# Transposing two token tiles by queue transfers set among the token loads, and the first tile's transposes by halves

## The chip, the cores and the metric

The kernel runs on one core of one Trainium2 chip. The metric is the device time of one execution in microseconds (us). The kernel before takes 1292.09 us (median of 3 runs, 1291.95 to 1292.39). Its granted TensorE clock is 1.000.

The engines are called as the profile calls them: PE is the matmul engine (TensorE), PEld its weight loads, DVE the vector engine, ACT the scalar engine, and SPq the sequencer that issues the transfers. "Landing" is the moment at which a transfer's data are complete.

## The reference, cut to what matters

```python
x = A_x                                                    # 2048 tokens x 1024, bf16
x = x + _A_ref(_layernorm(x), A_wqkv, A_wo)                # attention over 8 dilated positions, 32 heads
x = x + _B_ref(_layernorm(x), B_w1, B_b1, B_w2, B_b2)      # token-mixing MLP, 3584 wide
x = x + _A_ref(_layernorm(x), A_wqkv, A_wo)                # the same two again
x = x + _B_ref(_layernorm(x), B_w1, B_b1, B_w2, B_b2)
# in _A_ref:  qkv = x @ wqkv ; ... ; o @ wo
```

Only the opening of the first attention block matters here: the tokens are loaded, normalised over their 1024 features, transposed so that the features lie on the partitions, and multiplied with the value part of `wqkv`.

## The kernel before: the parts that matter

There are 16 token tiles of 128 tokens, called k. A list per engine gives the order of the opening's operations. `x_load` and `w_load` are loads of 256 KB each; `S_`, `A_` are the statistics on DVE; `R_` the reciprocal root on ACT; `N_` the normalisation on DVE. A tile is transposed either by PE (`tr`, eight 128x128 transposes into PSUM, followed by two ACT copies `C_` into `hT`) or by one queue transfer that transposes (`T_`). `V_` is the projection, 16 matmuls a tile, and `E_` the ACT copy of its result.

```python
        def tr(k):
            tps[k] = psm.tile([P, KD, P], BF16, name="m", tag="m")
            for kt in range(KD):
                r = nc.tensor.transpose(tps[k][:, kt, :], (xc[k] if k < 2 else xs[k])[:, kt * P:(kt + 1) * P], ident[:])
            return r

        def C_(k, hf):
            ks = slice(hf * KD // 2, (hf + 1) * KD // 2)
            return nc.scalar.copy(out=hT[:, ks, cols(*order[k])], in_=tps[k][:, ks, :])

        def T_(k):
            return nc.sync.dma_start_transpose(out=hT[:, :, cols(*order[k])], in_=xs[k])
        # ... [cut] all loads are issued first: x0, x1, w0..w3, x2, w4, w5, x3, w6, w7, x4 ... x15
        pe = [(tr, 0), (W_, 1), *VV(0, 0), (tr, 1), *VV(0, 1, 2), *VV(1, 0, 1, 2)]
        for kt in range(3, 6):
            pe += [*VV(0, kt), *VV(1, kt)]
        pe += [(tr, 2), *VV(0, 6, 7), *VV(1, 6, 7), (V_, 2, 0, a8), (tr, 3), (V_, 2, 1, a8), (tr, 4)]
        pe += [(V_, k, n, a8) for k in range(3, NT) for n in range(NDC)]
        # ... [cut]
        sp = [(T_, k) for k in (*range(np_, 10), 0, 1, *range(10, NT))] + [(load_biases,)]     # np_ = 5
```

So tiles 0 to 4 are transposed by PE, tiles 5 to 15 by the queue, after all loads. (Tiles 0 and 1 are only centred at first; the queue transposes them again later, scaled, for the query and key matmuls.) The queue's instructions run in the order of the list `sp`; a `T_` that waits for its normalisation holds up everything after it.

The softmax here doesn't subtract the row's maximum and nothing guards it: scores larger than these inputs give would overflow.

## Time and profile before

| | before |
|---|---|
| median, range | 1292.09 us, 1291.95 to 1292.39 (3 runs) |
| span of the profiled run | 1290.6 us |
| PE busy | 99% of the span |
| end of the opening (first query/key matmul, L383) | 64.32 us |

From the page: span, and busy time of each engine (share of the span, number of instructions).

```profile
span 1290.6 us, 19407 instructions
...
PE 1273.7 (99%) x8282; PEld 592.7 (46%) x8438; DVE 417.5 (32%) x854; ACT 370.9 (29%) x613; POOL 2.4 (0%) x15
```

PE is the bound. A change of the opening pays only if PE reaches the end of the opening earlier. The next lines are the timeline of PE (start, duration, engine, line, operation, out<-in, shape, how many; in brackets how long PE was idle before it and what ended that). Times of merged groups run to the end of the last matmul's pipeline, so they overlap a little; read the starts.

```profile
6.81 0.60 PE L267 MATMUL s<-wv,hT 128*128 128x512 bf16 x2 [0.46 <-ACT hT L261]
7.70 0.62 PE L256 MATMUL m<-ident,xc 128*128 128x128 bf16 x8 [0.29 <-DVE xc L238]
...
15.08 1.89 PE L267 MATMUL s<-wv,hT 128*128 128x512 bf16 x8
16.81 0.61 PE L256 MATMUL m<-ident,x 128*128 128x128 bf16 x8
17.25 1.89 PE L267 MATMUL s<-wv,hT 128*128 128x512 bf16 x8
18.98 0.61 PE L256 MATMUL m<-ident,x 128*128 128x128 bf16 x8
19.43 3.62 PE L267 MATMUL s<-wv,hT 128*128 128x512 bf16 x15
22.88 3.62 PE L267 MATMUL acc<-wv,hT 128*128 128x512 bf16 x16
...
64.32 7.07 PE L383 MATMUL m<-hT,wqk 128*128 128x512 bf16 x32
```

L256 is a PE transpose, L267 a projection matmul, L383 the first query/key matmul. Tile 3's transposes take 16.81 to 17.25 us and tile 4's 18.98 to 19.43 us; PE has no idle time near them (no bracket). The two small holes stand at the very start: before tile 0's projection (0.46 us) and before tile 1's transposes (0.29 us). Tile 4's projection, the first into the buffer `acc` after tile 1's, starts at 22.88 us.

The queue's side: the timeline of SPq.

```profile
7.57 8.54 SPq L219 DMA_DIRECT2D x<-in_A_x_dram  x12
22.21 24.16 SPq L279 DMA_TRANSPOSE hT<-x  x13
```

And from the view of line L279, the time from issue to landing of these 13 queue transposes.

```profile
DMA to landing us min/median/max: 3.0/3.6/5.0
```

All loads are issued by 16.1 us (7.57 + 8.54), and the first queue transpose follows at 22.21 us, just as the last load lands (22.24 us). It landed 3.2 us after issue.

### The profile page before, as it was taken

The page shows a single profiled execution, that of the slowest core. Times are in us where ns is not written, and L with a number is a line of the kernel's source. Part 1 is how long each engine was busy: PE and PEld are TensorE (multiplying, and loading weights), DVE is VectorE, ACT ScalarE, POOL GpSimd, SP SyncE. Part 2 cuts the span into 40 slices and gives each one's busy share as a digit, 9 for nine tenths or more (in the row PEclk, how much of TensorE's full clock was granted, in tenths as well). Part 3 has the DMA queues.
Part 4 walks back from the last instruction along what each step waited for, and adds up shares of the span by engine and source line. Part 5 has one row for each costly group of instructions (what it writes and reads, how often), then busy time and mean ns, then how long its engine had stood idle before and what let it go on. Part 6 is the DMA issues. An engine that isn't in the chain of part 4 may idle for free.

```text
span 1290.6 us, 19407 instructions
## 1 busy us (share of the span) xinstructions
PE 1273.7 (99%) x8282; PEld 592.7 (46%) x8438; DVE 417.5 (32%) x854; ACT 370.9 (29%) x613; POOL 2.4 (0%) x15
## 2 busy tenths in 40 slices
PE   9999999999999999999999999999999999999999
PEld 4444444444444444444444444444444444444444
DVE  6566777820000022322300677688000000111111
ACT  5366664541111110000023666645311111000000
POOL 0000000000000000000000000000000000000000
PEclk9999999999999999999999999999999999999999
DMA  6711123642222244465410111247423222334331
GB/s 223 112 46 48 50 83 124 208 139 82 66 82 75 57 117 132 132 165 131 132 32 1 48 49 51 80 150 219 116 66 92 71 61 82 100 106 138 116 92 33
DMA packets 201990, 126.07 MB, mean 98 GB/s; under 512 B 42160, under 2 KB 181680, under 8 KB 201904
## 3 DMA queue, kind: packets, MB, share of 16 engines
q1 hardware_dynamic: 201904, 124.82, 34.1%
q8 instruction: 66, 1.08, 0.3%
q14 instruction: 20, 0.16, 0.0%
HBM read 96.48 MB, written 16.78 MB: 88 GB/s over the span
## 4 chain that ended last, share of the span: by engine, by line
PE 98%; issue 1%; DMA 0%; DVE 0%; SPq 0%
PE m L383 17%; PE s L625 15%; PE s L578 15%; PE m L498 9%; PE acc L578 7%; PE m L578 7%; PE acc L625 7%; PE m L625 7%; PE m L368 4%; PE s L267 3%; PE s L414 2%; PE acc L267 1%; PE acc L449 1%; PE acc L453 1%; DMA x<-in_A_x_dram 0%
## 5 line engine op out<-in xcount | busy, mean ns | idle before, releaser
L625 PEld LDWEIGHTS <-w 128*128 128x128 bf16 x1820 | 177.0, 98 | 210.1
L578 PEld LDWEIGHTS <-w 128*128 128x128 bf16 x1792 | 175.3, 98 | 211.5
L383 PE MATMUL m<-hT,wqk 128*128 128x512 bf16 x963 | 223.3, 379 | 6.2 <-issue 4.6
L578 PE MATMUL s<-h,w 128*128 128x512 bf16 x878 | 201.2, 379 | 0.8
L625 PE MATMUL s<-g,w 128*128 128x512 bf16 (+1 forms) x912 | 201.0, 374 | 0.7
L627 DVE SCALAR_TENSOR_TENSOR xo<-s,b_sb,xs 128x512 bf16<-128x512 f32 (+1 forms) x33 | 24.4, 739 | 532.9 <-PE s L625 528.7
L383 PEld LDWEIGHTS <-wqk 128*128 128x128 bf16 x1024 | 95.2, 98 | 118.0 <-issue 10.7
L429 DVE TENSOR_TENSOR Pm<-pc,band 32x640 bf16<-32x640 bf16 x256 | 123.6, 483 | 56.2 <-ACT pc L417 49.4
L498 PE MATMUL m<-wo,oT 128*128 128x512 bf16 x500 | 110.6, 379 | 0.8 <-issue 0.3
L578 PE MATMUL acc<-h,w 128*128 128x512 bf16 x440 | 103.1, 379 | 0.5
L625 PE MATMUL acc<-g,w 128*128 128x512 bf16 x436 | 99.6, 379 | 0.5
L578 PE MATMUL m<-h,w 128*128 128x512 bf16 x438 | 98.5, 379 | 0.5
L625 PE MATMUL m<-g,w 128*128 128x512 bf16 (+1 forms) x436 | 96.9, 376 | 0.6
L176 ACT ACTIVATE ln<-mv,eps 128x1 f32<-128x1 f32 x64 | 18.9, 295 | 225.2 <-DVE mv L184 184.9
L498 PEld LDWEIGHTS <-oT 128*128 128x128 bf16 x512 | 49.6, 98 | 60.3 <-issue 1.3
L585 ACT ACTIVATE g<-s,b_sb 128x1024 bf16<-128x1024 f32 x28 | 31.2, 1114 | 158.2 <-PE s L578 146.4
L394 DVE COPY qB<-qs 32x512 bf16<-32x512 bf16 x136 | 38.2, 281 | 95.3 <-ACT qs L390 94.0
L368 PE MATMUL m<-wv,hT 128*128 128x512 bf16 x251 | 55.2, 379 | 0.3
L417 ACT ACTIVATE pc<-s,shift 128x640 bf16<-128x640 f32 x64 | 51.2, 800 | 11.7 <-PE s L414 11.7
L390 ACT CAST qs<-m 128x512 bf16<-128x512 f32 x64 | 37.5, 586 | 48.3 <-PE m L383 47.2
L387 ACT CAST kT<-m 128x512 bf16<-128x512 f32 x64 | 37.5, 586 | 46.4 <-PE m L383 46.4
L505 DVE TENSOR_TENSOR xn<-m,xr 128x512 bf16<-128x512 f32 x64 | 44.2, 690 | 16.9 <-PE m L498 16.4
(67 smaller groups left out, 683.0 us busy)
## 6 DMA issues: line engine op xcount, KB each, us to landing
w<-in_B_w_dram SPq DMA_DIRECT2D x56, 512.0 KB, 3.7
w<-in_B_w_dram SPq DMA_DIRECT2D x64, 448.0 KB, 4.4
wqk<-in_A_wqkv_dram SPq DMA_DIRECT2D x16, 512.0 KB, 5.2
xa<-xn SPq DMA_DIRECT2D x32, 256.0 KB, 2.2
xs<-xa SPq DMA_DIRECT2D x32, 256.0 KB, 3.1
wo<-in_A_wo_dram SPq DMA_DIRECT2D x8, 512.0 KB, 5.3
xr<-in_A_x_dram SPq DMA_DIRECT2D x16, 256.0 KB, 3.3
xb<-xo SPq DMA_DIRECT2D x16, 256.0 KB, 2.9
```

Of the source, the lines that this page charges most:

```text
L267: r = nc.tensor.matmul(pss_[k][:, n, :], lhsT=hT[:, kt, cols(*order[k])], rhs=wv[kt // 2][:, kt % 2, n * 512:(n + 1) * 512], start=(kt == ...
L368: nc.tensor.matmul(ps[:], lhsT=hT[:, kt, cols(c, i)], rhs=wv[kt // 2][:, kt % 2, n * 512:(n + 1) * 512], start=(kt == 0), stop=(kt == KD - 1))
L383: mm = nc.tensor.matmul(ps[:], lhsT=wts[part][:, kt, (g % 2) * P:(g % 2 + 1) * P], rhs=hT[:, kt, lo:lo + 512], start=(kt == 0), stop=(kt = ...
L387: nc.scalar.copy(out=kT[u % 2][:, ls], in_=ps[:])
L390: nc.scalar.copy(out=qs[:], in_=ps[:])
L394: nc.vector.tensor_copy(out=qB[u % 2][hp, h, ls], in_=qs[hp, :])
L417: nc.scalar.activation(out=pc[:].rearrange("p (n t) h k -> p n (t h k)", n=2), in_=ss[:, :, 0:2 * HG * GW], func=ACT.Exp, scale=scale, bia ...
L429: mm = nc.vector.tensor_tensor(out=Pm[rp, :, s0:s0 + HB, r * KG:r * KG + GW].rearrange("p h t k -> p t h k"), in0=pc[rp], in1=mk, op=ALU.mult)
L498: mm = nc.tensor.matmul(ps[:], lhsT=oT[g][:, cols(c, i)], rhs=wo[n][g // 4][:, g % 4, :], start=(g == 0), stop=(g == NG - 1))
L505: return nc.vector.tensor_tensor(out=xn[:, xs_], in0=pss_["o", n][:], in1=xr[:, xs_], op=ALU.add)
L578: nc.tensor.matmul(pairs[fl][0][dc], lhsT=wt[c][:, i, fl * P:(fl + 1) * P], rhs=h2[c][i][:, dc * 512:(dc + 1) * 512], start=(k == 0), stop ...
L625: nc.tensor.matmul(ap, lhsT=w2t[ft // HF][:, ft % HF, c::DIL], rhs=g[ft // GF][:, ft % GF, lo:lo + w], start=(ft == 0), stop=(ft == FT - 1))
```

## The change

The intent: tiles 3 and 4 leave PE too. Their queue transposes can't stand after all the loads, because PE would need the tiles before that, so they are set between the later loads. In passing, `tr` and `C_` go by halves with an own PSUM tile for each half, so that the copy of tile 0's first half need not wait for the transposes of its second. The diff, cut to its core:

```diff
@@ start_up
-        def tr(k):
-            tps[k] = psm.tile([P, KD, P], BF16, name="m", tag="m")
-            for kt in range(KD):
-                r = nc.tensor.transpose(tps[k][:, kt, :], ...)
+        def tr(k, hf):
+            tps[k, hf] = psm.tile([P, KD // 2, P], BF16, name="m", tag="m")
+            for j in range(KD // 2):
+                lo = (hf * KD // 2 + j) * P
+                r = nc.tensor.transpose(tps[k, hf][:, j, :], ...)
             return r
         def C_(k, hf):
-            return nc.scalar.copy(out=hT[:, ks, cols(*order[k])], in_=tps[k][:, ks, :])
+            return nc.scalar.copy(out=hT[:, ks, cols(*order[k])], in_=tps[k, hf][:])
@@ orders   [cut: the warm-up matmuls get a 128x128 tile of zeros that is filled first]
-        pe += [(tr, 2), *VV(0, 6, 7), *VV(1, 6, 7), (V_, 2, 0, a8), (tr, 3), (V_, 2, 1, a8), (tr, 4)]
-        pe += [(V_, k, n, a8) for k in range(3, NT) for n in range(NDC)]
+        pe += [(tr, 2, 0), (tr, 2, 1), *VV(0, 6, 7), *VV(1, 6, 7)]
+        pe += [(V_, k, n, a8) for k in range(2, NT) for n in range(NDC)]
-        act = [..., (R_, 2), (C_, 2, 0), (C_, 2, 1), (R_, 3), (E_, 0), (E_, 1), (R_, 4), (C_, 3, 0), (C_, 3, 1), (E_, 2),
-               (C_, 4, 0), (C_, 4, 1), (R_, 5), (E_, 3), (R_, 6)]
+        act = [..., (R_, 2), (R_, 3), (C_, 2, 0), (C_, 2, 1), (R_, 4), (E_, 0), (R_, 5), (E_, 1), (R_, 6), (E_, 2), (E_, 3)]
-        sp = [(T_, k) for k in (*range(np_, 10), 0, 1, *range(10, NT))] + [(load_biases,)]
+        sp = [(x_load, 0, halves), (x_load, 1), ...,   # as before up to
+              (x_load, 4), (x_load, 5), (x_load, 6), (T_, 3), (x_load, 7), (x_load, 8),
+              (T_, 4), (x_load, 9), (x_load, 10), (x_load, 11), (T_, 5), (x_load, 12), (x_load, 13), (T_, 6), (x_load, 14),
+              (x_load, 15), (T_, 7), (T_, 8), (T_, 9), (T_, 0), (T_, 1), *((T_, k) for k in range(10, NT)), (load_biases,)]
```

More of the change, by code (lines that the diff above doesn't have):

```diff
@@ L116 @@
     make_identity(nc, ident[:])
+    warm = const.tile([P, P], BF16, name="warm")
+    nc.vector.memset(warm[:], 0.0)
     eps1 = const.tile([P, 1], FP32, name="eps1")
@@ L206, in start_up @@
     def start_up(v, wv):
-        np_ = 5
         xc = [x2(f"xc{k}") for k in range(2)]
-        warm = x2("warm", [P, 512])
-        nc.vector.memset(warm[:], 0.0)
         xs, tps, pss_, mvs, sts, rss = {}, {}, {}, {}, {}, {}
@@ L251, in N_ @@
             return r
-        def tr(k):
-            tps[k] = psm.tile([P, KD, P], BF16, name="m", tag="m")
-            for kt in range(KD):
-                r = nc.tensor.transpose(tps[k][:, kt, :], (xc[k] if k < 2 else xs[k])[:, kt * P:(kt + 1) * P], ident[:])
+        def tr(k, hf):
+            tps[k, hf] = psm.tile([P, KD // 2, P], BF16, name="m", tag="m")
+            for j in range(KD // 2):
+                lo = (hf * KD // 2 + j) * P
+                r = nc.tensor.transpose(tps[k, hf][:, j, :], (xc[k] if k < 2 else xs[k])[:, lo:lo + P], ident[:])
             return r
@@ L279, in T_ @@
             return nc.sync.dma_start_transpose(out=hT[:, :, cols(*order[k])], in_=xs[k])
-        wm = m_tile()
+        wm = s_tile()
         def W_(n):
             for _ in range(n):
-                r = nc.tensor.matmul(wm[:], lhsT=warm[:, 0:P], rhs=warm[:], start=True, stop=True)
+                r = nc.tensor.matmul(wm[:, 0, :].rearrange("p (n q) -> p n q", q=P), lhsT=warm[:],
+                                     rhs=warm[:].unsqueeze(1).to_broadcast([P, 4, P]), start=True, stop=True)
             return r
@@ L293, in start_up @@
         chain_("ACT", ln_exp_table)
-        chain_("SP", x_load, 0, halves)
-        chain_("SP", x_load, 1)
-        for kt in range(4):
-            chain_("SP", w_load, kt)
-        chain_("SP", x_load, 2)
-        chain_("SP", w_load, 4)
-        chain_("SP", w_load, 5)
-        chain_("SP", x_load, 3)
-        chain_("SP", w_load, 6)
-        chain_("SP", w_load, 7)
-        for k in range(4, NT):
-            chain_("SP", x_load, k)
         def VV(k, *kts):
@@ L310, in start_up @@
         a8 = range(KD)
-        pe = [(tr, 0), (W_, 1), *VV(0, 0), (tr, 1), *VV(0, 1, 2), *VV(1, 0, 1, 2)]
+        pe = [(tr, 0, 0), (tr, 0, 1), (W_, 1), *VV(0, 0), (tr, 1, 0), (tr, 1, 1), *VV(0, 1, 2), *VV(1, 0, 1, 2)]
         for kt in range(3, 6):
             pe += [*VV(0, kt), *VV(1, kt)]
-        pe += [(tr, 2), *VV(0, 6, 7), *VV(1, 6, 7), (V_, 2, 0, a8), (tr, 3), (V_, 2, 1, a8), (tr, 4)]
-        pe += [(V_, k, n, a8) for k in range(3, NT) for n in range(NDC)]
-        act = [(Ma, 0, halves[1]), (C_, 0, 0), (C_, 0, 1), (C_, 1, 0), (C_, 1, 1), (R_, 0), (R_, 1), (R_, 2), (C_, 2, 0), (C_, 2, 1),
-               (R_, 3), (E_, 0), (E_, 1), (R_, 4), (C_, 3, 0), (C_, 3, 1), (E_, 2), (C_, 4, 0), (C_, 4, 1), (R_, 5), (E_, 3), (R_, 6)]
+        pe += [(tr, 2, 0), (tr, 2, 1), *VV(0, 6, 7), *VV(1, 6, 7)]
+        pe += [(V_, k, n, a8) for k in range(2, NT) for n in range(NDC)]
+        act = [(Ma, 0, halves[1]), (C_, 0, 0), (C_, 0, 1), (C_, 1, 0), (C_, 1, 1), (R_, 0), (R_, 1), (R_, 2), (R_, 3), (C_, 2, 0),
+               (C_, 2, 1), (R_, 4), (E_, 0), (R_, 5), (E_, 1), (R_, 6), (E_, 2), (E_, 3)]
         rs = [(R_, k) for k in range(7, NT)]
@@ L338, in start_up @@
         dve.append((cast_biases,))
-        sp = [(T_, k) for k in (*range(np_, 10), 0, 1, *range(10, NT))] + [(load_biases,)]
+        sp = [(x_load, 0, halves), (x_load, 1), *((w_load, kt) for kt in range(4)), (x_load, 2), (w_load, 4), (w_load, 5),
+              (x_load, 3), (w_load, 6), (w_load, 7), (x_load, 4), (x_load, 5), (x_load, 6), (T_, 3), (x_load, 7), (x_load, 8),
+              (T_, 4), (x_load, 9), (x_load, 10), (x_load, 11), (T_, 5), (x_load, 12), (x_load, 13), (T_, 6), (x_load, 14),
+              (x_load, 15), (T_, 7), (T_, 8), (T_, 9), (T_, 0), (T_, 1), *((T_, k) for k in range(10, NT)), (load_biases,)]
         qs = {"PE": pe, "ACT": act, "DVE": dve, "SP": sp}
-        need = {cast_biases: lambda: (load_biases,) in done, R_: lambda k: k in mvs, N_: lambda k, h: k in rss, tr: lambda k: (N_, k) in done if k > 1 else (M_, k) in done and (k == 1 or (Ma, k) in done),
-                B_: lambda k: k in mvs, M_: lambda k, h: k in mvs, Ma: lambda k, h: (B_, k) in done, C_: lambda k, hf: k in tps,
+        need = {cast_biases: lambda: (load_biases,) in done, R_: lambda k: k in mvs, N_: lambda k, h: k in rss, tr: lambda k, hf: (N_, k) in done if k > 1 else (M_ if k or not hf else Ma, k) in done,
+                S_: lambda k, cc: (x_load, k) in done,
+                B_: lambda k: k in mvs, M_: lambda k, h: k in mvs, Ma: lambda k, h: (B_, k) in done, C_: lambda k, hf: (k, hf) in tps,
                 V_: lambda k, n, kts: ((C_, k, kts[-1] * 2 // KD) in done or (T_, k) in done), E_: lambda k: (V_, k, 1) in done and (k > 1 or k in rss),
```

## The prediction

> **What bounds the kernel.** TensorE. The page gives PE 99% of a 1290.6 us span; the chain that ended last is 98% PE. In stretches of 5 us PE is busy 4.95 to 5.00 us from 10 us on, right through the opening's value projection (until 64.3 us). Only the first 8 us have holes: in the timeline PE starts at 1.38 us and waits 0.18, 0.46 and 0.29 us before tile 0's transposes, its first projection and tile 1's transposes. The change can gain only by taking PE work away or by shortening those holes.
>
> **Removed.** Tiles 3 and 4 lose eight PE transposes each: 16.81 to 17.25 and 18.98 to 19.43 us in the timeline, 0.89 us where PE has no gap. (56 ns each; the Trainium skill, "TensorE: Matmul & The Clock Gate", Part 1, states 55.6 ns start to start for 128 columns warm; this trace agrees.) All of it is on the chain. Four ScalarE copies of 0.59 us go too; ScalarE has slack.
>
> **Tile 0 by halves.** The first copy (6.17 us) no longer waits for all eight transposes, but for ScalarE's own centring of the second half (4.96 to 5.68): start near 5.75, first projection near 6.4 instead of 6.81. But then come tile 1's transposes, which in the chain of waits hang on tile 1's load (landed 5.57), statistics and centring, and start at 7.70. None of that moves. The hole before 7.70 grows to about 0.7 us: gain 0 (at most 0.1). The warm-up matmuls start 0.3 us earlier: gain 0.
>
> **Added and moved.** Thirteen queue transposes become fifteen. Those of before land 3.0 to 3.2 us after issue with nothing else in flight, up to 5.0 otherwise, and hold the issuer 1.23 to 1.35 us.
> - Tile 3: normalisation waits for its scale, now computed before tile 2's copies: estimate done at 15.05 (15.64 before). Loads up to tile 6 landed by 15.07, so transfers are idle: landing near 18.25; needed when tile 2's projection ends, 15.08 + 3.45 = 18.53. Slack 0.2 to 0.3 us, thin.
> - Tile 4: issued near 17.2 behind the loads of tiles 7 and 8 (0.68 us each at the rate seen), landing 20.5 to 21.5; needed at 21.98.
> - Tile 5: lands 23.5 to 24.5; needed at 25.4. Later ones have more slack. The last token load lands near 25 us instead of 22; DVE, at 2 us a tile, hides that.
> - Tile 2's copies stand behind tile 3's scale: the first ends near 15.0, needed at 15.08: stall 0 to 0.1 us.
>
> **Sum.** -0.89 us, +0 to 0.2 us of new waits: about -0.8 us, 0.06%; the spread before was 0.44 us. Predicted 1291.3 us, range 1290.3 to 1292.3. Faster by over 2%: 0.005; within 2%: 0.99; slower: 0.005.
>
> **What would show it.** PE timeline: no transposes after tile 2's; tile 3's projection starts at 18.5 (19.43 before), the query/key matmuls at 63.4 to 63.6 (64.32). Tile 1's transposes still near 7.70, the hole before them 0.7 us; tile 0's first copy at 5.75. PE waits on transfers into hT at most 0.2 us in total. Everything later is the same, shifted.
>
> **What would make it wrong.** A queue transpose among loads lands over 5 us after issue (no run yet shows one there; the skill, "DMA: Bandwidth & Descriptors", Rules for kernel authors, says a transpose next to ordinary transfers needs nothing), so tile 3 or 4 stalls PE by 0.5 us or more and eats the gain. Or the first 8 us shift: tile 1's load lands some tenths differently, or full clock is granted later than before.

## The result, and the profile after

| | before | after |
|---|---|---|
| median, range | 1292.12 us, 1291.95 to 1292.39 (6 runs) | 1292.40 us, 1291.72 to 1292.88 (6 runs) |
| ratio | | 1.0001, 95% interval 0.9988 to 1.0014 |
| span of the profiled run | 1290.6 us | 1290.4 us |
| first query/key matmul | 64.32 us | 64.30 us |

A ratio is the mean time of one kernel's runs over that of the other's in the same rounds, so it is not quite the ratio of the medians quoted. The median is 0.1 us above the upper end of the predicted range; a second set of five runs gave 1292.07 us. The expected gain of 0.8 us is not there. The predicted range, 1290.3 to 1292.3 us, also holds the time of the kernel before, so the time alone could hardly have refuted the prediction; what tests it are the moments that it foretold in the timeline of PE.

The timeline of PE after:

```profile
6.41 0.60 PE L267 MATMUL s<-wv,hT 128*128 128x512 bf16 x2
7.76 0.62 PE L256 MATMUL m<-ident,xc 128*128 128x128 bf16 x8 [0.75 <-DVE xc L237]
...
15.14 7.07 PE L267 MATMUL s<-wv,hT 128*128 128x512 bf16 x32
22.85 3.63 PE L267 MATMUL acc<-wv,hT 128*128 128x512 bf16 x16 [0.64 <-DMA hT<-x]
...
64.30 7.07 PE L375 MATMUL m<-hT,wqk 128*128 128x512 bf16 x32
```

The transposes of tiles 3 and 4 are gone: from 15.14 us on, 32 matmuls run in one piece, the projections of tiles 2 and 3. The hole before tile 1's transposes is 0.75 us as predicted, with no gain from the halves. And there is a new wait: tile 4's projection starts at 22.85 us, only 0.03 us earlier than before. Two projections of 3.455 us (one is 22.88 - 19.43 = 3.45 in the kernel before) after 15.14 would have ended at 22.05, so about 0.80 us is lost there. (The profile shows 0.64 us idle because it draws a matmul 0.379 us long, though the next one starts 0.216 us after it.) The view of PE's waits from 8 to 64 us has one line (us in total, times, longest):

```profile
PE acc L267 <- DMA hT<-x: 0.6, 1, 0.6
```

The view of line L279 for the one transfer issued at 17.43 us, tile 4's, names who waited for it and its time to landing:

```profile
  PE acc L267: 0.6, 1
...
DMA to landing us min/median/max: 5.4/5.4/5.4
```

Tile 4's queue transpose landed 5.4 us after issue, not the 3.0 to 3.2 us of an undisturbed one. The timeline of SPq shows how it stood in the queue:

```profile
14.86 1.36 SPq L279 DMA_TRANSPOSE hT<-x  x1
16.28 1.05 SPq L218 DMA_DIRECT2D x<-in_A_x_dram  x2
17.43 1.24 SPq L279 DMA_TRANSPOSE hT<-x  x1
```

Tile 3's transpose is issued at 14.86, then the loads of tiles 7 and 8 (16.28), then tile 4's (17.43). From the landing records of the trace, which list 16 parts for each transfer:

```
after:   issue   first part   last part
  T_3    14.86     17.88        18.03     (3.17 after issue)
  x7     16.28     18.68        19.54
  x8     16.89     19.59        21.91
  T_4    17.43     22.63        22.80     (5.38 after issue; PE's tile 4 starts at 22.85)
```

Tile 8's load is drawn out: three of its 16 parts landed by 20.38 us, the other 13 only from 21.75 us on. At the same time something else uses the transfer engines. This is the view of queues for 20 to 21 us (kind: packets, MB, share of 16 engines):

```profile
q1 hardware_dynamic: 177, 0.05, 187.0%
q8 instruction: 1, 0.02, 6.0%
```

The q8 packet is an instruction fetch of 16384 B, from 20.04 to 21.00 us. The Trainium skill, "Runtime: NRT & Kernel Launch", Instruction fetch mechanics, says that each engine's instruction memory is refilled in blocks of 16 KiB by a queue of its own, and calls the cost mostly hidden; the size agrees with the trace. 177 packets of q1 that began in this microsecond add up to 187% of what 16 engines have in it: they took far longer than normal. By the packet records 17 packets of 256 B, in this stretch those of a queue transpose, took up to 1.56 us instead of 0.018 us, and all ended at 21.8 us, just before tile 8's load was complete (21.91).

So there were two suspects for the late landing, and chance as a third.

- **Q, the place in the queue:** the transpose stood behind two loads.
- **F, the fetch:** an instruction fetch held up a part of the transfers, and a queue transpose is complete only when the last of its 16 parts has landed.
- **R, chance:** landing times of transposes scatter, and the next run shows another.

### The profile page after: what moved, and what is told of

Read it like the earlier page. It is cut to its first block, busy times and chain, and to the rows that moved or that the text cites. A ratio compares the mean times of both kernels' runs of the same rounds, so it can differ in the third digit from the quotient of the medians.

```text
span 1290.4 us, 19531 instructions
## 1 busy us (share of the span) xinstructions
PE 1285.0 (100%) x8422; PEld 591.8 (46%) x8422; DVE 417.4 (32%) x854; ACT 368.7 (29%) x609; POOL 2.4 (0%) x15
## 4 chain that ended last, share of the span: by engine, by line
PE 98%; DMA 1%; DVE 0%; SPq 0%; ACT 0%; issue 0%
PE m L375 18%; PE s L617 15%; PE s L570 15%; PE m L490 9%; PE acc L570 7%; PE acc L617 7%; PE m L570 7%; PE m L617 7%; PE m L360 4%; PE s L267 2%; PE s L406 2%; PE acc L441 1%; PE acc L267 1%; PE acc L445 1%; DMA x<-in_A_x_dram 0%; DMA hT<-x 0%
## 5 line engine op out<-in xcount | busy, mean ns | idle before, releaser
L375 PE MATMUL m<-hT,wqk 128*128 128x512 bf16 x1024 | 231.8, 380 | 0.0
L178 ACT ACTIVATE ln<-mv,eps 128x1 f32<-128x1 f32 x64 | 18.8, 294 | 228.7 <-DVE mv L186 184.9
```

The costliest lines, as they stand in the source:

```text
L375: mm = nc.tensor.matmul(ps[:], lhsT=wts[part][:, kt, (g % 2) * P:(g % 2 + 1) * P], rhs=hT[:, kt, lo:lo + 512], start=(kt == 0), stop=(kt = ...
```

## The experiments

Eight runs followed, in two sets of four, each set on one chip with its own runs of the kernel before.

**What makes the runs comparable.** The load of tile 1 landed at 5.57 us in the first profile of before and 5.63 in that after, but at 4.76 to 5.65 in the later ones, and the dense part of PE starts with it: tile 1's transposes start at 7.2 to 7.3 us when it lands by 5.2 (later in the two kernels that put work in front of them: 7.39 and 7.87). This is not the change's doing, since the kernel before does it too (below). So the table has the first query/key matmul also counted from the start of tile 1's transposes. The rest of the span, from that matmul on, is 1226.1 to 1226.3 us in all ten profiles, so nothing after the opening differs by more than 0.2 us.

| kernel | tile 1's transposes | tile 4's projection | query/key | query/key from tile 1's | landing of T_4 after issue | median (range) us |
|---|---|---|---|---|---|---|
| before | 7.70 | 22.88 | 64.32 | 56.62 | (PE) | 1292.12 (1291.95 to 1292.39) |
| after | 7.76 | 22.85 | 64.30 | 56.54 | 5.38 | 1292.40 (1291.72 to 1292.88) |
| before_again | 7.24 | 22.42 | 63.86 | 56.62 | (PE) | 1292.28 (1292.00 to 1292.45) |
| after_again | 7.28 | 22.62 | 64.08 | 56.80 | 5.52 | 1292.07 (1291.62 to 1292.25) |
| halves_only | 7.21 | 22.39 | 63.83 | 56.62 | (PE) | 1291.99 (1291.92 to 1293.22) |
| t3_only | 7.61 | 22.34 | 63.78 | 56.17 | (PE) | 1291.80 (1291.55 to 1292.18) |
| fetch_early | 7.87 | 22.16 | 63.60 | 55.73 | 4.57 | 1291.62 (1291.31 to 1291.66) |
| loads_ahead | 7.21 | 21.50 | 62.94 | 55.73 | 3.07 | 1291.21 (1291.17 to 1291.45) |
| loads_ahead_fill | 7.39 | 21.55 | 62.98 | 55.59 | 3.06 | 1291.22 (1291.03 to 1291.88) |
| fetch_hits | 7.78 | 23.46 | 64.90 | 57.12 | 3.90 | 1292.72 (1291.81 to 1293.11) |

### 1. after_again: the changed kernel once more

No edit.

> The changed kernel unaltered, a second profile and more times. Both theories (Q: tile 4's queue transpose lands late because it stands behind the loads of tiles 7 and 8; F: because a 16384 B instruction fetch at about 20 us freezes its packets for about 1.55 us) expect tile 4's transpose to land near 22.8 us, 5.4 us after issue, the fetch at about 20.0 us, PE waiting 0.6 us before tile 4's projection and the query/key matmuls at 64.3 us. A rival R (the late landing was a chance of one run) expects a landing before 21.9 us and no wait. Median 1292.1 to 1292.5 us by Q and F.

Measured: tile 4's transpose landed 5.52 us after issue, and PE waited again, as its timeline shows.

```profile
7.28 0.62 PE L256 MATMUL m<-ident,xc 128*128 128x128 bf16 x8 [0.38 <-DVE xc L237]
...
22.62 3.63 PE L267 MATMUL acc<-wv,hT 128*128 128x512 bf16 x16 [0.89 <-DMA hT<-x]
```

The view of L279 for this transfer, issued at 17.06 us:

```profile
DMA to landing us min/median/max: 5.5/5.5/5.5
```

The fetch came at 20.47 us. In the landing records tile 8's load was complete at 20.09 this time, but tile 4's transpose landed its first part at 21.01 and its last at 22.58: now a single late part was in the transpose itself (15 of the 16 had landed by 21.18), and no 256 B packet took over 0.5 us before that. Chance alone (R) loses ground: the late landing came twice, of the same size, though the loads were some tenths earlier. PE would have been ready at 14.66 + 6.91 = 21.57 us, so it lost 1.05 us here; and it could have borne a landing 4.51 us after issue (4.62 us in the first profile, 22.05 - 17.43). From tile 1's transposes, the opening was 56.80 us, 0.18 us longer than before.

### 2. loads_ahead: no load between the two transposes

```diff
-  (x_load, 6), (T_, 3), (x_load, 7), (x_load, 8), (T_, 4), (x_load, 9), ...
+  (x_load, 6), (x_load, 7), (x_load, 8), (T_, 3), (T_, 4), (x_load, 9), ...
```

> The loads of tiles 7 and 8 are issued before tile 3's queue transpose, so that tile 4's follows tile 3's with nothing between. Q and F: tile 4's is issued near 16.9 us, lands near 20.0 us (before or at the fetch), PE doesn't wait for it, tile 4's projection starts at 22.05 us, query/key matmuls at 63.5 us instead of 64.3; time 0.8 us below the changed kernel's, about 1291.4 us. R (landing times of queue transposes vary by chance): no systematic gain. Tile 3's must still land before 18.6 us; if the two loads delay it PE waits there instead.

Measured, timeline of PE:

```profile
7.21 0.62 PE L256 MATMUL m<-ident,xc 128*128 128x128 bf16 x8 [0.28 <-DVE xc L237]
...
14.59 7.07 PE L267 MATMUL s<-wv,hT 128*128 128x512 bf16 x32
21.50 3.62 PE L267 MATMUL acc<-wv,hT 128*128 128x512 bf16 x16
...
62.94 7.07 PE L375 MATMUL m<-hT,wqk 128*128 128x512 bf16 x32
```

The wait is gone: PE starts tile 4's projection 6.91 us after tile 2's, two projections without a gap. The view of L279 for the transfer issued at 16.01 us:

```profile
DMA to landing us min/median/max: 3.1/3.1/3.1
```

The median is 1291.21 us, and all five runs (1291.17 to 1291.45) lie below every run of the kernel before (1291.95 to 1292.55). The ratio to before is 0.9993 with an interval of 0.998 to 1.0005: the interval alone would not show a gain. The timelines do: counted from tile 1's transposes the opening is 55.73 us, 0.89 us shorter than before, which is just the sixteen transposes of 0.056 us that PE no longer does. This confirms the arithmetic of the gain, and that tile 4's late transpose gave it back. Tile 3's transpose stood behind the same two loads here and was issued (14.02 us) before they had landed (14.86 and 15.51), yet it took only 3.22 us: two loads issued over 3 us earlier cost nothing. Q is about loads issued just before the transpose. The run doesn't tell Q from F: here tile 4's transpose is out of the way of both (it landed at 19.08; the fetch came at 19.61).

### 3. fetch_early: the queue as in the changed kernel, the fetch moved away

```diff
+        def D_(n):
+            for _ in range(n):
+                r = nc.tensor.matmul(wm[0:16, 0, 0:16], lhsT=warm[:, 0:16], rhs=warm[:, 0:16], start=True, stop=True)
+            return r
-        pe = [..., *VV(0, 0), (tr, 1, 0), (tr, 1, 1), ...
+        pe = [..., *VV(0, 0), (D_, 26), (tr, 1, 0), (tr, 1, 1), ...
```

> The changed kernel with 26 tiny matmuls (16x16, results unused) put into the hole before tile 1's transposes, so that TensorE's instruction stream is 52 instructions ahead and the 16384 B fetch should come about 5.6 us earlier, at 14 to 15 us, before any queue transpose moves data. Tile 4's transpose still stands behind two loads. F: it lands about 1.5 us earlier, near 21.2 us, PE doesn't wait, tile 4's projection starts at 22.05 us (plus any spill of the tiny matmuls over the hole, at most 0.3 us). Q: it lands near 22.8 us as before and PE waits 0.6 us. If the fetch doesn't move, the run says nothing between them and the fetch isn't tied to the count of PE instructions.

Measured: the view of queues for 13 to 14 us now holds the fetch (13.69 us by the record).

```profile
q8 instruction: 1, 0.02, 7.1%
```

It moved by over 6 us when nothing but 52 PE instructions was added, so it is a fetch of PE's instructions. The view of L279 for tile 4's transpose, issued at 17.18 us:

```profile
DMA to landing us min/median/max: 4.6/4.6/4.6
```

And the timeline of PE:

```profile
7.14 0.80 PE L291 MATMUL s<-warm 128*16 128x16 bf16 x26
...
15.25 7.07 PE L267 MATMUL s<-wv,hT 128*128 128x512 bf16 x32
22.16 3.62 PE L267 MATMUL acc<-wv,hT 128*128 128x512 bf16 x16
```

Tile 4's transpose landed 4.6 us after issue, at 21.74, and PE did not wait: 22.16 - 15.25 is again 6.91 us. The opening from tile 1's transposes is 55.73 us, as in loads_ahead. (The tiny matmuls spilled by about 0.6 us: tile 1's transposes started at 7.87 us, with a load that landed at 4.79.) All five runs, 1291.31 to 1291.66 us, lie below every run of the kernel before. So without the fetch at 20 us PE did not wait. The spill helped: it put PE's need off, so that a landing 22.16 - 17.18 = 4.98 us after issue could be borne. With the 4.51 to 4.62 us of the changed kernel, 4.57 would have been just at the edge, a wait of 0.06 us at most instead of 0.8 to 1.05. F had expected about 1.5 us less, but the landing came only about 0.8 to 0.95 us earlier (4.57 against 5.38 and 5.52). The rest, 4.57 against the 3.07 of loads_ahead, goes with Q: two loads issued just ahead cost 1.5 us. By the packet records even here 15 of the 256 B packets took up to 0.98 us and ended together at 20.4 to 20.5 us, where tile 8's load landed (20.52 to 20.73). How much belongs to each is not shown by this one profile. Tile 6's transpose also stands right behind two loads, in all seven profiles of the changed queue, with no 16384 B fetch in flight: it landed 4.16 us after issue here and in the first profile of the changed kernel, and 4.42 to 5.33 us in the other five. So loads just ahead cost 1 us or more in each of these, and a difference of 0.8 to 0.95 us between two profiles is within that scatter. What a fetch does by itself is tested in run 7.

### 4. halves_only: the halves without the moved tiles

```diff
 (kernel before)
-  (tr, 0) ... (tr, 4)            tps[k], one PSUM tile for eight transposes
+  (tr, 0, 0), (tr, 0, 1) ...     tps[k, hf], one for each four; warm-up matmuls into an s tile
```

> The kernel before with transposes and copies by halves in own PSUM tiles alone; tiles 3 and 4 still transposed by PE. My prediction: tile 0's first copy at 5.76 us (6.17), first projection at 6.4 us (6.81), the hole before tile 1's transposes grows to 0.75 us and they start at 7.7 us as before: query/key matmuls at 64.3 us, time within 0.1 us of before. The rival (halves shorten the opening) expects the query/key matmuls 0.3 to 0.4 us earlier, at 63.9 us.

Measured: first query/key matmul at 63.83 us, which looks like the rival's 63.9. But tile 1's load landed at 4.96 us in this run, so the comparison with 64.32 was not fair. The next run settles it.

### 5. before_again: the kernel before once more

No edit.

> The kernel before, unaltered, for a second profile. Tile 1's load landed at 5.57 and 5.63 us in the first two profiles and at 4.76 to 5.15 us in the next four, and the start of the dense part moved with it (7.2 to 7.3 us instead of 7.7). If the halves gain nothing, the kernel before starts tile 1's transposes near 7.25 us whenever that load is early (the first projection, 6.81 to 7.24, then gates it), and reaches the query/key matmuls near 63.85 us, as the halves alone did (63.83). If the halves gain 0.3 us or more, it stays near 7.7 and 64.3 us with an early load too.

Measured, timeline of PE of before_again:

```profile
7.24 0.62 PE L256 MATMUL m<-ident,xc 128*128 128x128 bf16 x8
...
63.86 7.07 PE L383 MATMUL m<-hT,wqk 128*128 128x512 bf16 x32
```

The same of halves_only:

```profile
7.21 0.62 PE L257 MATMUL m<-ident,xc 128*128 128x128 bf16 x8
...
63.83 7.07 PE L384 MATMUL m<-hT,wqk 128*128 128x512 bf16 x32
```

With an early load (5.11 us) the kernel before reaches the same point, and from tile 1's transposes both take 56.62 us. In these two profiles the halves gain 0.03 us at most. The times leave more room: four of the five runs of halves_only lie between 1291.92 and 1292.12 us (one at 1293.22), with 1292.26 the median of before in the same set. A gain of 0.2 to 0.3 us can't be excluded by them; no profile shows where it would be.

### 6. t3_only: half of the move

```diff
 (changed kernel)
+        pe: (V_, 2, ...), (tr, 4, 0), (tr, 4, 1), (V_, 3, ...)      act: ... (E_, 1), (C_, 4, 0), (C_, 4, 1), (R_, 6) ...
-        sp: ... (x_load, 7), (x_load, 8), (T_, 4), (x_load, 9) ...
+        sp: ... (x_load, 7), (x_load, 8), (x_load, 9) ...
```

> The changed kernel with tile 4 back on PE transposes; only tile 3 goes through the queue, ahead of the loads of tiles 7 on. It removes half of the PE work, 0.44 us, and leaves out the transfer that landed late. Theory (the change's gain is 0.44 us a tile, and tile 4's late landing gave all of it back): PE waits for no transfer, tile 4's transposes run right after tile 2's projection or tile 3's, query/key matmuls 0.4 us earlier than in the kernel before at the same start of tile 1's transposes. Time about 0.4 us below before. Rival (a queue transpose costs elsewhere what it saves on PE): no gain.

Measured, timeline of PE:

```profile
7.61 0.62 PE L256 MATMUL m<-ident,xc 128*128 128x128 bf16 x8 [0.47 <-DVE xc L237]
...
18.44 0.61 PE L256 MATMUL m<-ident,x 128*128 128x128 bf16 x8
...
63.78 7.07 PE L376 MATMUL m<-hT,wqk 128*128 128x512 bf16 x32
```

PE waits for no transfer, and the opening from tile 1's transposes is 56.17 us: 0.45 us less than before, one tile's worth. The median is 1291.80 us, 0.38 below that of before in the same set (1292.18).

### 7. fetch_hits: no load ahead, but the fetch moved onto a transpose

```diff
 (loads_ahead)
-        pe = [..., *VV(0, 0), (tr, 1, 0), ...
+        pe = [..., *VV(0, 0), (D_, 9), (tr, 1, 0), ...          # nine tiny matmuls, as in fetch_early
```

> The loads-ahead kernel (tile 4's queue transpose lands 3.1 us after issue there, moving data from 17.0 to 18.6 us; fetch at 19.6 us) with 9 tiny matmuls in the early hole, so that the 16384 B fetch should come 2.0 to 2.2 us earlier, at 17.4 to 17.6 us, in the middle of that transpose. F: its 256 B packets freeze for about 1 to 1.5 us while the fetch lasts, and it lands 4.0 to 4.6 us after issue though no load stands before it; PE still doesn't wait (slack over 2 us). Q alone: it lands 3.1 us after issue as without.

Measured: the fetch came at 17.08 us, and tile 1's load was late this time (5.65 us), so it fell on tile 3's transpose, not tile 4's. What it did there is plainer than what was expected. The view of queues from 17 to 18 us holds the fetch and nothing else:

```profile
DMA packets 1, 0.02 MB, mean 16 GB/s; under 512 B 0, under 2 KB 0, under 8 KB 0
...
q8 instruction: 1, 0.02, 6.0%
```

By the packet records, 21 packets of 256 B that began at 16.7 us or soon after ended together at 18.8 us; the longest took 2.14 us. Tile 3's transpose, issued at 14.88, landed at 19.95, 5.07 us after issue, though the loads ahead of it were done before the freeze (tile 8's had landed at 16.16), and though the same order took 3.22 us in loads_ahead and 3.21 in loads_ahead_fill. In the six other profiles that have it, it took 3.16 to 3.22 us. The timeline of PEld:

```profile
19.99 4.00 PEld L267 LDWEIGHTS <-hT 128*128 128x128 bf16 x20 [1.71 <-DMA hT<-x]
```

And of PE:

```profile
15.16 3.62 PE L267 MATMUL s<-wv,hT 128*128 128x512 bf16 x16
19.99 3.63 PE L267 MATMUL s<-wv,hT 128*128 128x512 bf16 x16 [1.21 <-ACT ln L178]
```

The weight load for tile 3 waited for this transfer until 19.99 us. (The line of PE itself names ACT as the releaser; that work had long been done.) PE lost about 1.4 us: tile 2's projection would have ended at 15.16 + 3.45 = 18.61. This profile is of the slowest of the four runs (1293.11 us); the others took 1291.81 to 1293.01, the median is 1292.72. In the profiled run nine tiny matmuls in an idle hole cost 1.4 us, through the moment of an instruction fetch. fetch_early, with 26 of them and the fetch at 13.69 us, is the control: its tile 3 landed 3.17 us after issue. The freeze began up to 0.4 us before the fetch's own packet; what the fetch does in that time the records don't show.

The traces at hand show the same effect again, without any experiment. The next 16384 B fetch comes at 39.6 to 45.9 us, when no token load is left and one queue transpose follows another. In all ten profiles 18 to 21 packets of 256 B then began between 0.1 us before that fetch and 0.3 us after its end, took up to 0.76 to 1.86 us, and ended within 0.05 us of each other. In the kernel before, the transpose issued at 39.83 us met it and took 4.97 us; in the changed kernel, where this fetch comes only at 45.64, the one issued at 39.82 took 3.63. So the "up to 5.0 otherwise" that the prediction quoted was already a transpose that had met a fetch. (A fetch is not the only cause: 256 B packets of up to 0.98 us stand in fetch_early at 19.5 us, with no such fetch near.)

### 8. loads_ahead_fill: an attempt at more

```diff
 (loads_ahead)
-        pe = [..., *VV(0, 0), (tr, 1, 0), (tr, 1, 1), *VV(0, 1, 2), ...
+        pe = [..., *VV(0, 0, 1), (tr, 1, 0), (tr, 1, 1), *VV(0, 2), ...
```

> A version meant to beat both: loads of tiles 7 and 8 ahead of the first queue transpose, and tile 0's projection with the second weight tile (two matmuls, 0.43 us) moved into the hole before tile 1's transposes. Expected against the loads-ahead kernel: tile 1's transposes not later than 0.1 us (7.2 to 7.3 us with an early load), a new gap of at most 0.2 us before tile 1's first projection, query/key matmuls 0.25 us earlier (62.7 us) with an early load and up to 0.43 us with a late one; time about 0.25 us below 1291.2, 1.2 us below before. If the hole is needed for something else (the second weight tile lands after 6.9 us) the gain is nil.

Measured: no gain. Tile 1's transposes started at 7.39 us instead of 7.21, and then tile 1's first projection (8.45, into `acc`) had to wait for its copy. The timeline of PE:

```profile
7.39 0.61 PE L256 MATMUL m<-ident,xc 128*128 128x128 bf16 x8
...
8.45 1.47 PE L267 MATMUL acc<-wv,hT 128*128 128x512 bf16 x6
...
62.98 7.07 PE L375 MATMUL m<-hT,wqk 128*128 128x512 bf16 x32
```

The hole before tile 1's transposes is only 0.28 us with an early load; filling it delayed the copy that the next step needs. The query/key matmuls started at 62.98 us (62.94 in loads_ahead), and the median is 1291.22 us (1291.21). loads_ahead stays the best version.

## Why the prediction was right or wrong

- **"All of it is on the chain" (0.89 us of PE transposes): right.** loads_ahead and fetch_early, where no transfer is late, are 0.89 us shorter from tile 1's transposes to the query/key matmuls; t3_only is 0.45 us shorter. The prediction took its 56 ns from the timeline and from the Trainium skill, "TensorE: Matmul & The Clock Gate", Part 1 (55.6 ns); these runs agree.
- **"Tile 0 by halves: gain 0": right by the profiles.** 56.62 us in halves_only and in both profiles of before. The first copy came at 5.76 us and the first projection at 6.41 us, and the hole before tile 1's transposes grew to 0.75 us, as written.
- **"Tile 3: landing near 18.25; needed 18.53": right.** It landed at 18.03 us and PE did not wait.
- **"Tile 4: issued near 17.2 behind the loads of tiles 7 and 8, landing 20.5 to 21.5; needed at 21.98": wrong, and this is the step that failed.** It was issued at 17.43 and landed at 22.80. The term, from issue to landing, was mis-sized: 3.3 to 4.3 us by the estimate, 5.38 and 5.52 measured. Two loads just ahead cost 1.5 us (4.57 us from issue to landing in fetch_early, 3.07 in loads_ahead), 0.3 us more than the upper end of my estimate. The other 0.8 to 0.95 us went away when an instruction fetch at 20 us was moved (one profile, so the size is uncertain); I had not thought of this fetch: it is in the trace of before as well (at 19.78 us), where the last token load then had a late part (first part 20.09, last 22.24), and nobody waited for that.
- **"+0 to 0.2 us of new waits": wrong in consequence.** It was 0.80 us in the first profile, and the sum of -0.89 and +0.80 is the result. The prediction named this failure (a transpose among loads landing over 5 us after issue) without giving it enough weight: the time was foretold as 1291.3 us and was 1292.40, the query/key matmuls at 63.4 to 63.6 us and came at 64.30.
- **"Tile 5: lands 23.5 to 24.5; needed at 25.4": too early, without consequence by luck.** It landed at 25.61, needed at 26.31 in the delayed course of PE; without tile 4's wait it would have been needed at 25.51 and come 0.1 us late.
- **"Tile 2's copies: stall 0 to 0.1 us": right.** PE had no gap there.
- **"Tile 1's load lands some tenths differently": it did, in later runs,** by up to 0.9 us, in kernels with and without the change. It moves the start by up to half a microsecond, as much as what was to be measured.

What stays open: which of the 16 engines carried the fetch, how much of tile 4's delay the fetch caused and how much the loads ahead, and why a fetch of about 1 us can hold a transpose for 1.5 to 2.1 us. In after_again the late part was in the transpose itself and not in the load ahead of it; the records don't give the engine of a packet, so the two courses can't be followed further.

## What to carry to other kernels

Before work is moved from the bound engine to a transfer queue, compare the moment at which the result is needed with the landing of a transfer that stands behind others, not with that of one alone; here 3.1 us became 4.2 to 5.3 behind two loads issued just before, and 5.4 to 5.5 where an instruction fetch came as well; the slack was 4.5 to 4.6. Order the queue by who needs what first: issuing two token loads 6.8 us earlier (9.52 instead of 16.28 us), ahead of the transposes, kept the whole gain (0.89 us in the timeline; 1291.21 us against 1292.26 for the kernel before in the same set). And when a difference of a microsecond in a thousand is sought, count from an event inside the opening, because the first loads land differently from run to run.

## What the Trainium skill lacked or had wrong

- "DMA: Bandwidth & Descriptors" (Rules for kernel authors) says that a transpose next to ordinary transfers needs nothing. For the result that agrees (every run was correct), but the rule says nothing of time: from issue to landing one 128x1024 transpose took 3.0 to 3.2 us undisturbed, 4.2 to 5.3 us right behind two loads of 256 KB, and 5.4 to 5.5 us where an instruction fetch came as well.
- "Runtime: NRT & Kernel Launch" (Instruction fetch mechanics) calls the cost of crossing a 16 KiB block mostly hidden. It was hidden from PE's own issue here, but not from the transfers: the first fetch of 16384 B took 0.96 to 1.13 us in the ten profiles, and a queue transpose that it met landed 5.07 us after issue instead of 3.2 and held PE for 1.4 us. No page says that a fetch can delay a transpose.
- No page says that the packets of a queue transpose freeze together when one part of the transfers is late: 256 B packets that normally take 0.018 us took up to 1.56 us (after) and 2.14 us (fetch_hits), and ended at the same moment.
